# One written list for all five engines in a sliding-window attention + gated MLP kernel, with casts on three engines and two more batches transposed by DMA

## The chip, the core and the metric

One Trainium2 chip, one core, one launch. The time is the device time of the launch in microseconds. A core has five engines that run their own instruction queues in order: PE (matrix products), ACT (scalar activations), DVE (vector), POOL (GpSimd) and SP (used here for transfers only). Transfers are issued from the queues of SP, ACT and POOL and run on 16 shared DMA engines. Products go to PSUM, eight banks of 512 fp32 columns.

## What is computed

Sliding-window attention with ALiBi slopes over 8 batches, 8 heads, 576 tokens of 64, and then an MLP over all 4608 tokens:

```python
def _attn_ref(q, k, v):                      # 8, 8, 576, 64
    window, scale = 128, 1.0 / np.sqrt(D)
    scores = scale * np.matmul(q, k.transpose(0, 1, 3, 2))
    rel = pos[:, None] - pos[None, :]
    bias = slopes[:, None, None] * (-np.abs(rel))
    mask = (rel >= 0) & (rel < window)
    scores = np.where(mask, scores + bias[None], -1e9)
    ...                                      # softmax over the last axis
    return np.matmul(attn, v)

def _moe_ref(x, w_in, w_out, beta):          # x: 4608 x 512
    h = x @ w_in                             # 512 x 2048
    g = h * (1.0 / (1.0 + np.exp(-beta * h)))
    return g @ w_out                         # 2048 x 512
```

## The kernel before

The attention of a batch works in blocks of 128 tokens (four full ones and a tail of 64). The MLP works in nine groups g of 512 tokens, so groups and batches don't line up: a group waits for the last attention block that it contains. All products are in bf16.

**Inputs.** `get` (line 207) and `get_pair` (line 218) load q, k and v as fp32 from the queue of SP into 14 staging buffers `fst`; `cast_pair` (235), `cast_qk` (228, 229) and `cast_v` (243) turn them into bf16 on POOL. For batches 0 and 1 the staged blocks (`bst`, four buffers) are transposed by PE (`TP`, 287; the tail in `TT`) and copied from PSUM to `QK` by DVE and ACT; from batch 2 on a DMA transposes them (`DT`, 413, on SP's queue). From batch 3 on v is loaded and cast in one transfer on POOL's queue (`get_v`, 250). The weights W1 and W2 come in four pieces each, on POOL's queue (258, 262). `QK` and `VS` are two deep, by batch parity.

**Attention.** Scores are `SP_` (324, 335) for batches 0 and 1 and `SC` (438) from batch 2 on; ACT takes the exponential into `pt` (342, 446), DVE multiplies in the ALiBi factor and mask (`factor`, 171, 176), PE multiplies with v (`PVP` 374, `PVB` 492 and 495), DVE divides by the row sum (`norm` 358 and 359, 499 and 500).

**Its output** `xn` must be transposed into `XT`, a ring of three groups. `X` (lines 503 to 535) does it: for batches 0 and 1 by PE; for batches 2 and 3 by four PE products with the identity (line 520) and a copy by ACT (line 523); for batches from `XDMA = 4` on by a DMA on SP's queue (line 512).

**MLP.** `Hm` (557) makes 128 rows of h for a group from four products of 128x512, `H` in what follows; ACT makes tanh (564) and DVE the gated product (565) into `gT` (two buffers). `OS` (588) makes a quarter of an output block from four such products, `O` in what follows; ACT halves the sum into `osb` (598) and `store` (606) sends it out from POOL's queue for groups below 3 and from ACT's later.

**Order.** The order on PE, SP and POOL is that of the program. A first part is written out by hand; after that `spread` places the attention steps `att` between the MLP's steps by weights, `jobs` and `blocks` place the loads and casts. ACT and DVE are written by hand until the first two H, then left to the scheduler. PSUM is held in pools that are opened and closed as the stages go by. `idle` and `calm` are products of zeros that keep PE running in the opening.

Of the kernel before, what the change touches and what calls it, by code (L numbers as in the profile page):

```python
# [15 lines left out]
P = 128  # L16


@with_exitstack
def kernel(  # L20
# [63 lines left out]
    psum_c = ctx.enter_context(tc.tile_pool(name="psum_c", bufs=1, space=bass.MemoryType.PSUM))  # L84
    psum_h = ctx.enter_context(tc.tile_pool(name="psum_h", bufs=2, space=bass.MemoryType.PSUM))
    trans = ExitStack()
    psum_t = trans.enter_context(tc.tile_pool(side="right", name="psum_t", bufs=2, space=bass.MemoryType.PSUM))
    SS = psum_c.tile([P, 2, 512], F32, name="SS")
    psum_c.seal()
    opening = ExitStack()  # L90
    psum_x = opening.enter_context(tc.tile_pool(name="psum_x", bufs=1, space=bass.MemoryType.PSUM))
    SX = psum_x.tile([P, 2, 512], F32, name="SX")
    late, gates = {"tick": 0}, {}
    spans = [SS]

    def span():

        spans.append(spans.pop(0))
        return spans[-1]

    def obank(name, tag=None):
        if tag is None:
            late["n"] = late.get("n", 0) + 1
            tag = "ops" if late["n"] % 2 else "h3"
        return late["o"].tile([P, DM], F32, name=name, tag=tag)[:]

    def after(ins, other):
        tc.add_manual_dep(
            ins.ins, other.ins.name,
            mybir.DependencyInfo(mybir.DependencyClass.Sync, mybir.DependencyReason.DATA),  # L110
            reason="gate",
        )

    def idle(n):
        for _ in range(n):
            nc.tensor.matmul(
                SS[:, 0, :], lhsT=zeros[:, 0:P], rhs=zeros[:], start=True, stop=True,
                skip_group_check=True)  # L120

    def constants():
# [4 lines left out]
        idle(8)  # L127
# [35 lines left out]
    def falls_late(i):  # L163
        to, a, w = ((0, 0, P), (128, 0, 64), (192, 0, P), (320, 1, 64), (384, 1, P))[i]
        after(nc.vector.tensor_copy(
            out=falls[:, :, to : to + w], in_=fall[:, :, a, 0:w]), gates[1, 4])

    def factor(pt, m, p):

        if m:  # L170
            nc.vector.tensor_tensor(  # L171
                out=pt[:], in0=pt[:], in1=falls[:, 2 * p : 2 * p + 2], op=ALU.mult)
            return
        t = (fallq if m is None else fall)[:, 2 * p]
        x = pt[:].rearrange("k e (a n q) -> k (e a) n q", a=2, n=2)
        nc.vector.tensor_tensor(  # L176
            out=x, in0=x, in1=bass.AP(tensor=t.tensor, offset=t.offset,
                                      ap=[list(t.ap[0]), [P, 4], [0, 2], [1, P]]), op=ALU.mult)
# [11 lines left out]
    def betas():  # L190
        bps = psum_t.tile([P, NFF], F32, name="bps", tag="t")
        nc.tensor.transpose(out=bps[:], in_=bflat[:], identity=identf[:])
        nc.vector.tensor_scalar_mul(beta_h[:], bps[:], 0.5)
# [7 lines left out]
    def get(what, b, sb):  # L201
# [5 lines left out]
        return nc.sync.dma_start(  # L207
# [4 lines left out]
    def get_pair(b, p):  # L212

        r = []
        for what, src in (("k", k), ("q", q)):
            f = fst_pool.tile([P, 2, 4, D], F32, name="fst", tag="fst")
            fs[what, b, "p", p] = f
            r.append(nc.sync.dma_start(  # L218
                out=f[:].rearrange("r h c d -> r h (c d)"),
                in_=src[b, 2 * p : 2 * p + 2, 0:FULL, :].rearrange("h (r c) d -> r h (c d)", c=4),  # L220
            ))
        return r[0]

    def cast_qk(b, sb):
        rows = ROWS[sb]
        t = bst_pool.tile([P, 2, H, D], BF16, name="bst", tag="bst")
        staged[b, sb] = t
        nc.gpsimd.tensor_copy(out=t[0:rows, 0], in_=fs.pop(("q", b, sb))[0:rows])  # L228
        return nc.gpsimd.tensor_copy(out=t[0:rows, 1], in_=fs.pop(("k", b, sb))[0:rows])  # L229

    def cast_pair(b, p):
        t = bst_pool.tile([P, 2, 4, 2 * D], BF16, name="bst", tag="bst")
        staged[b, "p", p] = t
        for i, what in ((1, "k"), (0, "q")):
            r = nc.gpsimd.tensor_copy(
                out=t[:, i].rearrange("r c (h d) -> r h c d", d=D),
                in_=fs.pop((what, b, "p", p))[:])
        return r

    def cast_v(b, sb):  # L240
        moved.add(("v", b, sb))
        rows = ROWS[sb]
        return nc.gpsimd.tensor_copy(  # L243
            out=VS[b % 2][0:rows, sb, :, 0:D], in_=fs.pop(("v", b, sb))[0:rows])
# [22 lines left out]
    pts, xns = {}, {}  # L267

    def calm(n):

        z = psum_h.tile([P, 512], F32, name="z", tag="hps")
        for _ in range(n):
            nc.tensor.matmul(
                z[:], lhsT=zeros[:, 0:P], rhs=zeros[:], start=True, stop=True,
                skip_group_check=True)

    def TP(b, p):
        src = staged.pop((b, "p", p))
        for i in (1, 0):
            if (b, p) == (0, 1):  # L280
                calm(1 + i)
            tps = psum_t.tile([P, FULL], BF16, name="tps", tag="t")
            to = tps[:].rearrange("d (c r) -> d c r", c=4)
            if i == 0:
                to = tps[:].rearrange("d (k c r) -> d c k r", k=4, c=4)
            for c in range(4):
                nc.tensor.transpose(out=to[:, c], in_=src[:, i, c], identity=ident[:])
            if i:
                nc.vector.tensor_copy(
                    out=QK[b % 2][:, 1, p, 0:FULL].rearrange("d (r c) -> d r c", c=4),  # L290
                    in_=tps[:].rearrange("d (c r) -> d r c", c=4))
            else:
                nc.scalar.copy(out=QK[b % 2][:, 0, p, 0:FULL], in_=tps[:])

    def TT(b):

        src = staged.pop((b, 4))
        tps = psum_t.tile([P, 2, NP, 64], BF16, name="tpt", tag="t")
# [7 lines left out]
        nc.scalar.copy(out=QK[b % 2][:, :, :, FULL:S], in_=tps[:])  # L306
# [6 lines left out]
    def SP_(b, vis, p):  # L313
        qk = QK[b % 2]
        sps = SX if vis == "B" else SS
        w = WIDTH[vis]
        biased = vis == "A" or p > 1
# [22 lines left out]
        pt = pt_pool.tile([P, 2, 512], BF16, name="pt", tag="pt")  # L340
        pts[b, vis, p] = pt
        nc.scalar.activation(out=pt[:, :, 0:w], in_=sps[:, :, 0:w], func=ACTF.Exp, scale=qscale)
        if vis == "B" and b and not biased:
            factor(pt, None, p)

    def room(b, shape):

        if b == 0:
            return psum_h.tile(shape, F32, name="pvh", tag="hps")[:]
        if "o" in late:  # L350
            return obank("pvo")[:, 0 : 4 * 66].rearrange("p (h x) -> p h x", x=66)
        return psum_t.tile(shape, F32, name="pv", tag="t")[:]
# [9 lines left out]
    def PVP(b, vis, p):  # L362
        vs = VS[b % 2]
        if vis == "A":
# [3 lines left out]
        pv = room(b, [P, 4, 66])  # L368
# [10 lines left out]
        norm(xn[:, q0 : q0 + 2, :].rearrange("p n (e d) -> p (n e) d", e=2), pv, P)  # L379

    def XP(b, p):
        xn = xns.pop((b, "p", p))
        xt = psum_t.tile([P, 4, P], F32, name="xtp", tag="t")
        for n in range(4):
            nc.tensor.matmul(xt[:, n, :], lhsT=xn[:, n, :], rhs=order[:], start=True, stop=True)
        (nc.vector.tensor_copy if (b, p) == (0, 3) else nc.scalar.copy)(
            out=XT[:, p, b * S : b * S + FULL], in_=xt[:].rearrange("d n q -> d (n q)"))

    def SCT(b):
        qk = QK[b % 2]  # L390
        for p in range(NP):
            for kb, at in ((4, 0), (3, 256)):
                for e in range(2):
                    nc.tensor.matmul(
                        SS[:, e, at + 64 * p : at + 64 * p + 64],
# [3 lines left out]
                    )  # L399
        nc.scalar.activation(  # L400
            out=PC[:, 0:1024].rearrange("p (e w) -> p e w", e=2), in_=SS[:], func=ACTF.Exp,
            scale=qscale)
        nc.vector.tensor_tensor(
# [5 lines left out]
    def DT(b, sb):  # L409
# [7 lines left out]
        if (b, sb) == (2, 0):  # L417
            after(r, w2[3])
# [3 lines left out]
    def SC(b, m, pp):  # L422
# [3 lines left out]
        spans.sort(key=lambda t: t is not SS)  # L426
        for p, sps in zip(pp, spans):
            for kb in ((0, 1), (2, 4, 3))[m]:
                at, then = COLS[kb]
                nq = {3: P + 64, 4: 64}.get(kb, 2 * P)  # L430
                for e in range(2):
                    o = sps[:, e, at : at + min(nq, 512 - at)]
                    if kb in (0, 2):
                        o = bass.AP(
                            tensor=o.tensor, offset=o.offset,
                            ap=[list(o.ap[0]), [then - at, 2], [1, P]],
                        )
                    nc.tensor.matmul(  # L438
                        o,
                        lhsT=qk[64 * e : 64 * e + 64, 1, p, P * kb : P * kb + P],  # L440
# [101 lines left out]
    def Hm(g, j, cs):  # L542
# [18 lines left out]
        if cs[-1] < NDM - 1:  # L561
            return
# [332 lines left out]
```

The softmax here doesn't subtract the row's maximum and nothing guards it: scores larger than these inputs give would overflow.

## Time and profile before

| | us |
|---|---|
| median of 3 runs | 325.4 (324.65 to 327.33) |
| span of the profiled execution | 324.0 |
| ACT busy in it | 194.1 (60%) |
| DVE busy in it | 183.1 (57%) |
| POOL busy in it | 98.8 (30%) |

The span runs from the first to the last instruction of the execution that was profiled. The products of PE overlap each other in the records, so that "mean ns of one" is longer than what one costs: 16 products of 128x512 in a row take 3.45 us on the chain of work, or 0.216 us each, while the mean of one is 379 ns.

The transfers of the page, with size and median time from issue to landing:

```profile
fst<-in_k_dram SPq DMA_DIRECT2D x32, 256.0 KB, 6.0
vs<-in_v_dram POOLq DMA_DIRECT2D x20, 128.0 KB, 6.1
W<-in_moe_w_in_dram POOLq DMA_DIRECT2D x4, 512.0 KB, 7.9
W<-in_moe_w_out_dram POOLq DMA_DIRECT2D x4, 512.0 KB, 12.8
```

### The profile page before, as it was taken

To read this page: it belongs to the slowest core of one execution; us is meant where nothing else is said; L and a number is where in the kernel's file an instruction comes from. 1 tells how busy PE (TensorE), PEld (TensorE's weight loads), DVE (VectorE), ACT (ScalarE), POOL (GpSimd) and SP (SyncE) were. 2 spreads that over 40 slices of the span, in tenths; PEclk is the share of its full clock that TensorE was granted. 3 is DMA by queue.
4 is the path that set the end of the run, shared out by engine and by line. 5 is a ranking of instruction groups with operands and counts; after the bars stand their busy time and mean duration, and the time that the engine had idled before them with its cause. 6 is when DMAs were issued, how large, how long until landed. Compare 5 with 4: busy or idle time off the path is not lost.

```text
span 324.0 us, 5988 instructions
## 1 busy us (share of the span) xinstructions
PE 312.7 (97%) x2297; PEld 153.3 (47%) x2297; DVE 183.1 (57%) x346; ACT 194.1 (60%) x283; POOL 98.8 (30%) x154
## 2 busy tenths in 40 slices
PE   8888999999999999999999999999999999999995
PEld 3454554443545454544454545444544455444443
DVE  5777877542548753785178717752775176335500
ACT  6857887635558865685467635845675465346511
POOL 4864820333873455356226232340000000000000
PEclk9999999999999999999999999999999999999999
DMA  7999999998999999999969994993222112110021
GB/s 221 252 263 238 176 196 196 215 199 162 214 181 208 222 208 139 230 217 148 257 153 196 150 245 94 211 138 107 18 65 60 65 18 65 46 62 32 10 90 65
DMA packets 147565, 48.84 MB, mean 151 GB/s; under 512 B 135360, under 2 KB 143824, under 8 KB 147536
## 3 DMA queue, kind: packets, MB, share of 16 engines
q1 hardware_dynamic: 115712, 32.39, 56.1%
q0 software_dynamic: 28624, 10.29, 26.1%
q10 hardware_dynamic: 3200, 5.78, 5.1%
q8 instruction: 18, 0.29, 0.4%
q14 instruction: 11, 0.09, 0.1%
HBM read 36.71 MB, written 9.44 MB: 142 GB/s over the span
## 4 chain that ended last, share of the span: by engine, by line
PE 69%; DMA 17%; SPq 6%; POOL 2%; ACT 2%; DVE 2%; issue 1%; POOLq 0%; DVEq 0%
PE ops L588 21%; PE hps L557 21%; PE hpo L557 10%; PE oph L588 7%; DMA fst<-in_v_dram 6%; DMA qkT<-bst 6%; SPq L207 3%; DMA fst<-in_q_dram 3%; DMA fst<-in_k_dram 2%; PE SS L438 2%; SPq L218 2%; PE ST L438 1%; PE SS L495 1%; PE SS L492 1%; POOL bst L229 1%
## 5 line engine op out<-in xcount | busy, mean ns | idle before, releaser
L588 PE MATMUL ops<-W,gT 128*128 128x512 bf16 (+1 forms) x464 | 109.7, 372 | 0.5 <-ACT osb L598 0.5
L565 DVE SCALAR_TENSOR_TENSOR gT<-sig,hps 128x512 bf16<-128x512 bf16 x100 | 67.6, 683 | 71.8 <-ACT sig L564 71.5
L557 PE MATMUL hps<-XT,W 128*128 128x512 bf16 x400 | 99.9, 379 | 0.3 <-DVE XT L533 0.3
L564 ACT ACTIVATE sig<-hps,beta_h 128x512 bf16<-128x512 f32 x100 | 68.1, 690 | 34.6 <-PE hps L557 33.2
L588 PEld LDWEIGHTS <-gT 128*128 128x128 bf16 x592 | 55.7, 98 | 61.6 <-issue 1.9
L557 PEld LDWEIGHTS <-W 128*128 128x128 bf16 x576 | 52.9, 98 | 60.8 <-issue 3.6
L228 POOL CAST bst<-fst 128x512 bf16<-128x512 f32 (+1 forms) x32 | 20.8, 650 | 74.4 <-DMA fst<-in_q_dram 42.4
L557 PE MATMUL hpo<-XT,W 128*128 128x512 bf16 x168 | 43.1, 379 | 0.0
L564 ACT ACTIVATE sig<-hpo,beta_h 128x512 bf16<-128x512 f32 x42 | 29.0, 690 | 16.9 <-PE hpo L557 16.9
L565 DVE SCALAR_TENSOR_TENSOR gT<-sig,hpo 128x512 bf16<-128x512 bf16 x42 | 28.6, 681 | 11.2 <-ACT sig L564 11.0
L598 ACT ACTIVATE osb<-ops 128x512 f32<-128x512 f32 (+1 forms) x28 | 16.6, 595 | 25.5 <-PE ops L588 25.5
L446 ACT ACTIVATE pt<-SS 128x1024 bf16<-128x1024 f32 x24 | 24.5, 1020 | 11.6 <-PE SS L438 11.1
L588 PE MATMUL oph<-W,gT 128*128 128x512 bf16 x128 | 29.3, 379 | 0.0
L229 POOL CAST bst<-fst 128x512 bf16<-128x512 f32 (+1 forms) x32 | 22.1, 690 | 15.6 <-DMA fst<-in_k_dram 15.0
L176 DVE TENSOR_TENSOR pt<-pt,fall 128x1024 bf16<-128x1024 bf16 x24 | 17.1, 712 | 14.8 <-ACT pt L446 14.8
L446 ACT ACTIVATE pt<-ST 128x1024 bf16<-128x1024 f32 x24 | 24.5, 1022 | 0.0
L171 DVE TENSOR_TENSOR pt<-pt,falls 128x1024 bf16<-128x1024 bf16 x24 | 18.8, 791 | 9.3 <-ACT pt L446 9.3
L250 POOL DMA_DIRECT2D vs<-in_v_dram x25 | 21.3, 869 | 0.2 <-issue 0.2
L598 ACT ACTIVATE osb<-oph 128x512 f32<-128x512 f32 x8 | 4.8, 597 | 21.1 <-PE oph L588 21.1
L495 PEld LDWEIGHTS <-pt 128*128 128x128 bf16 x240 | 14.8, 97 | 4.2
L243 POOL CAST vs<-fst 128x512 bf16<-128x512 f32 (+1 forms) x15 | 10.5, 703 | 15.9 <-DMA fst<-in_v_dram 15.9
L438 PEld LDWEIGHTS <-qkT 64*128 64x128 bf16 x240 | 8.9, 94 | 12.5 <-issue 12.0
(102 smaller groups left out, 257.8 us busy)
## 6 DMA issues: line engine op xcount, KB each, us to landing
fst<-in_k_dram SPq DMA_DIRECT2D x32, 256.0 KB, 6.0
fst<-in_q_dram SPq DMA_DIRECT2D x32, 256.0 KB, 5.3
out_dram<-osb ACTq DMA_DIRECT2D x22, 256.0 KB, 2.0
fst<-in_v_dram SPq DMA_DIRECT2D x12, 256.0 KB, 5.4
out_dram<-osb POOLq DMA_DIRECT2D x12, 256.0 KB, 5.2
vs<-in_v_dram POOLq DMA_DIRECT2D x20, 128.0 KB, 6.1
W<-in_moe_w_in_dram POOLq DMA_DIRECT2D x4, 512.0 KB, 7.9
W<-in_moe_w_out_dram POOLq DMA_DIRECT2D x4, 512.0 KB, 12.8
```

The source lines that it names most:

```text
L171: nc.vector.tensor_tensor(out=pt[:], in0=pt[:], in1=falls[:, 2 * p : 2 * p + 2], op=ALU.mult)
L228: nc.gpsimd.tensor_copy(out=t[0:rows, 0], in_=fs.pop(("q", b, sb))[0:rows])
L229: return nc.gpsimd.tensor_copy(out=t[0:rows, 1], in_=fs.pop(("k", b, sb))[0:rows])
L250: return nc.gpsimd.dma_start(out=VS[b % 2][0:rows, sb, :, 0:D], in_=v[b, :, P * sb : P * sb + rows, :].rearrange("h p d -> p h d"))
L438: nc.tensor.matmul(o, lhsT=qk[64 * e : 64 * e + 64, 1, p, P * kb : P * kb + P], rhs=qk[64 * e : 64 * e + 64, 0, p, P * kb : P * kb + nq], ...
L446: nc.scalar.activation(out=pt[:], in_=sps[:], func=ACTF.Exp, scale=qscale)
L495: nc.tensor.matmul(o, lhsT=weights(b, qb, h, 0), rhs=vs[:, qb, h, 0 : D + 1], start=qb == 0, stop=True, skip_group_check=True)
L557: nc.tensor.matmul(hps, lhsT=W1[:, c, bass.ts(j, P)], rhs=XT[:, c, c0 : c0 + TOKG], start=(c == 0), stop=(c == NDM - 1),)
L564: gates[g, j] = nc.scalar.activation(out=sig[:], in_=hps, func=ACTF.Tanh, scale=beta_h[:, j : j + 1])
L565: gates["gT"] = nc.vector.scalar_tensor_tensor(out=gts[g][:, j, :], in0=sig[:], scalar=1.0, in1=hps, op0=ALU.add, op1=ALU.mult)
L588: nc.tensor.matmul(ops_[:, cols], lhsT=gT[:, j, i * P : i * P + P], rhs=W2[:, j, cols], start=(j == 0), stop=(j == NFF - 1),)
L598: nc.scalar.mul(o, ops_[:, cols], 0.5)
```

## The change

The order of all five engines now comes from one text, `PLAN`, of 1300 steps; each step is a name and its indices (batch, block or pair, group, PSUM bank) and an engine letter where there is a choice (p POOL, v DVE, a ACT, s SP). A loop reads it and issues the steps one after the other. Each earlier function is split into its PE part and its ACT or DVE part, so that the two can stand at different places. PSUM is one tensor of eight banks, and each PE step names its bank.

- Casts: all 95 were on POOL; 44 still are, 31 are on DVE and 20 on ACT, in the opening and in the later batches.
- `X` by PE is left for the tails of batches 0 and 1 only. Batches 2 and 3 go through `XD`, ten DMA transposes more on SP's queue. The 40 products of line 520 and the ten copies by ACT are gone. All other products stay, 16 of zeros among them.
- Output copies: 24 on ACT and 13 on DVE (before 36 and 1). Stores: 17 on POOL's queue, 13 on SP's and 7 on ACT's (before 12, 3 and 22).
- Order in the opening: before the first H there are, besides batch 0, seven of the eight pair transposes of batch 1 and four of its eight score steps. The loads of batch 1's q and k stand between batch 0's v. The first W1 piece is issued on POOL after the cast of batch 0's third v block. The last scores of batch 7 come before group 7.
- One step, `A`, gets a factor by DVE as a possibility (`MA`); the list doesn't use it.

```diff
+PLAN = """
+k.s:0:1 k.s:0:0 const beta:2 k.s:0:2 ck.p:0:1 ck.p:0:2 q.s:0:0 q.s:0:1 k.s:0:3 cq.p:0:1 ck.v:0:0
+Rk:0:2:3 z:2:2 Rq:0:1:0 Rk:0:0:6 Rk:0:1:5 rq.a:0:1 rk.a:0:0 cq.v:0:0 ones fr:2 ck.p:0:3 q.s:0:2
+q.s:1:0 q.s:0:3 Rq:0:0:0 cq.v:0:2 k.s:1:0 gv.s:0:3 Rk:0:3:7 rk.a:0:2 k.s:1:3 cq.p:0:3 Rq:0:2:1
...
+B:0:2:3:1 EA:0:2 EB:0:0 fr:7 MB:0:0 cq.v:1:0 q.s:1:1 A:0:0:1:1 z:2:6 B:0:3:5:1 w1:0 EB:0:2 EA:0:0
+A:0:1:2:1 k.s:1:1 cv.v:0:1 Rq:1:0:0 Rk:1:0:4 VB:0:2:1 EB:0:3 EA:0:1 rk.a:1:0 rq.v:1:0 A:0:3:5:1
...
+cK.v:2:0 d:1:3 H:1:4:1 gq.s:2:3 gk.s:2:1 D:2:4 cQ.v:2:2 d:1:8 w2:2 d:1:7 d:1:0 H:1:5:3 a:1:4
+cQ.a:2:0 H:1:10:2 D:2:0 gk.s:2:3 d:1:13 d:1:4 cQ.a:2:1 a:1:5 cK.a:2:1 a:1:1 a:1:14 cK.v:2:2 D:2:1
+cQ.a:2:3 O:0:0:0:4 gv.s:2:2 O:0:3:0:6 d:1:14 d:1:5 O:0:3:1:6 fl:4 H:1:15:1 H:1:2:0 d:1:1 a:1:11
...
+cK.p:3:2 O:1:1:0:1 V:2:2:5 n:2:2 cQ.v:3:2 O:1:2:0:0 oc.a:1:0 O:1:2:1:0 O:1:1:1:1 cK.a:3:0 V:2:4:3
+O:1:2:2:0 O:1:1:2:1 O:1:3:0:2 XD:2:0 V:2:3:6 gq.s:4:4 n:2:3 O:1:2:3:0 O:1:1:3:1 XD:2:2 gk.s:3:4
+D:3:1 H:2:0:7 n:2:4 a:2:0 d:2:0 D:3:2 cK.v:3:4 H:2:4:6 cK.p:3:3 oc.a:1:1 cQ.p:3:3 H:2:7:5 a:2:4
...
+"""
...
+    PS = psum.tile([P, 8, 512], F32, name="PS")
...
+    def move(eng, out, in_):
+        (nc.scalar.copy if eng is nc.scalar else eng.tensor_copy)(out=out, in_=in_)
...
-        nc.gpsimd.tensor_copy(out=t[0:rows, 0], in_=fs.pop(("q", b, sb))[0:rows])
-        return nc.gpsimd.tensor_copy(out=t[0:rows, 1], in_=fs.pop(("k", b, sb))[0:rows])
...
+        move(eng, staged[b, sb][0:rows, "qk".index(what)], fs.pop((what, b, sb))[0:rows])
...
-            nc.scalar.copy(out=XT[:, :, tok0 : tok0 + n1], in_=xt[:, :, 0:n1])
...
+    def XD(b, qb):
+        xnv = xns.pop((b, qb))[:].rearrange("p h d -> p (h d)")
+        for r0, r1, at in pieces(b, qb):
+            nc.sync.dma_start(out=XT[:, :, at : at + r1 - r0], in_=xnv[r0:r1], transpose=True)
...
+    def OC(eng, g, i, part=None):
...
+        if eng is nc.scalar:
+            nc.scalar.mul(o, src, 0.5)
+        else:
+            eng.tensor_scalar_mul(o, src, 0.5)
...
+    with tc.manual_schedule(engines={ENG.PE, ENG.SP, ENG.Pool, ENG.Activation, ENG.DVE}):
+        for step in PLAN.split():
+            name, *at = step.split(":")
+            name, _, eng = name.partition(".")
+            STEPS[name](*([ENGINES[eng]] if eng else []), *map(int, at))
```

Names of the list: k, q, gv, gq, gk are loads; ck, cq, cv, cQ, cK casts; Rk, Rq transposes of a pair by PE, rk, rq their copies; A, B and S scores, EA, EB and E their exponentials, MB and M the factors; VA, VB and V the products with v, nA, nB and n the divisions; XP the transposes of an output by PE with their copies xc; D and XD the DMA transposes; H, a, d the hidden products with tanh and gated product; O, oc, st the output products, copies and stores; z products of zeros.

## The prediction

> **What bounds the kernel now.** I read the page's busy times first, then stretches of the span, then what PE waited for, then the groups that the change touches.
>
> ```profile
> PE 312.7 (97%) x2297; PEld 153.3 (47%) x2297; DVE 183.1 (57%) x346; ACT 194.1 (60%) x283; POOL 98.8 (30%) x154
> ...
> PEclk9999999999999999999999999999999999999999
> DMA  7999999998999999999969994993222112110021
> ```
> ```profile
> 0.00:10.00 10.00, 7.93 (x48) 3.60 (x49) 6.72 (x28) 7.12 (x15) 5.19 (x16) 1.00 0.84 233
> 10.00:20.00 10.00, 8.90 (x124) 5.03 (x124) 7.04 (x21) 7.21 (x11) 8.81 (x15) 1.00 1.19 272
> 20.00:30.00 10.00, 9.32 (x65) 4.30 (x64) 7.74 (x15) 7.37 (x13) 3.34 (x5) 1.00 1.09 229
> 30.00:40.00 10.00, 9.19 (x99) 4.68 (x100) 7.83 (x18) 7.87 (x12) 8.84 (x15) 1.00 1.02 188
> 40.00:50.00 10.00, 9.12 (x113) 5.26 (x109) 7.12 (x18) 7.85 (x13) 2.01 (x4) 1.00 1.23 196
> ...
> 300.00:324.00 24.00, 20.07 (x109) 10.37 (x106) 4.46 (x7) 6.21 (x10) 0.00 (x0) 0.99 0.15 55
> ```
>
> PE is the bound: 97% busy at a full clock (1.00 in every stretch but the last). Its idle time is 324.0 - 312.7 = 11.3 us. The five stretches to 50 us hold 2.07 + 1.10 + 0.68 + 0.81 + 0.88 = 5.5 of it, the last stretch 3.9 (the last product, its copy and its store), and all between only 1.8. So the change can gain by fewer PE products, by a denser opening, and by little else. Beside PE the DMA engines are busy until 220 us (the row DMA; a share over 1 means that packets overlap in the records); this is what can turn into a new bound. The waits, in total, times and longest, name the small holes:
>
> ```profile
> POOL bst L228 <- DMA fst<-in_q_dram: 42.4, 12, 12.8
> ...
> PE tps L287 <- POOL bst L235: 1.8, 4, 0.7
> ...
> PE SS L438 <- DMA qkT<-bst: 1.3, 3, 0.5
> ```
>
> The last two are PE's and cost time. The first is POOL's: it stands before its casts until the load is there (and 15.0 us more, in 18 waits, for k). Nobody else stands with it.
>
> **Part 1: the output transposes of batches 2 and 3.** These are the products removed, and the transfers of the same kind that stay:
>
> ```profile
> L520 PE MATMUL ST<-ident,xn 128*128 128x128 bf16 x16 | 1.6, 220 | 0.5 <-DVE xn L500 0.5
> L520 PE MATMUL SS<-ident,xn 128*128 128x128 bf16 x16 | 1.5, 219 | 0.0
> ...
> L520 PE MATMUL ST<-ident,xn 64*128 64x64 bf16 x8 | 0.6, 192 | 0.0
> ```
> ```profile
> qkT<-bst SPq DMA_TRANSPOSE x30, 4.7
> ...
> XT<-xn SPq DMA_TRANSPOSE x21, 2.8
> ```
>
> Removed from PE: 1.6 + 1.5 + 0.6 = 3.7 us busy and 0.5 us of waits, all on the bound: **-4.2 us**. Removed from ACT: ten copies, some 5.6 us, hidden. Added: ten transposes on SP's queue. The nearest row is the same transfer for later batches: 1.19 us of SP's queue and 2.8 us to landing. Here a rule speaks for the change: the Trainium skill ("Advanced Engine Details and Errata", section X-Bar Transpose (TRN2)) has transposing transfers as fast as plain ones, at 350 to 400 GB/s, so that a block of 128 KB would take some 0.4 us (estimate: 128 KB by that rate). The row says 2.8 us in the quiet late stage, and 4.7 for the double size among loads; by the rule ten cost 4 us of transfer, by the row 28, or up to 47. I take the row. It is hidden if the group that needs the block starts later than that: between the last product with v of block (2, 2), V:2:2, and the first product of group 2 the list has eight O and two V. An O is 4 x 0.216 = 0.86 us and a V is 0.48 by the starts of successive groups in the timeline: 8 x 0.86 + 2 x 0.48 = 7.9 us. The division takes 0.2 + 0.69 of it, the transfer 2.8 to 4.7: 2 us are over, and SP's queue has only one load (gq.s:4:4) just ahead of it. For batch 3's three blocks in group 3 the lead in PE work is 6 to 10 us. I cost it at nothing; if the cover is gone PE waits 1 to 3 us at H of groups 2 and 3 each.
>
> **Part 2: the opening.** Same PE work up to group 1, less holes or more? Three things set the first H, at 19.4 us before. (a) Loads: the first twelve landed by 14.7 us (the cast of the last v block starts then), one each 1.0 us. In the new list batch 0's v blocks are loads 11, 13, 14 and 15, so the last v lands at 17 to 18, not 15. (b) W1's first piece is issued on POOL after the cast of load 14, near 18 us (10.5 before); with the page's 7.9 us to landing it is there at 26. (c) ACT: up to the last copy before the first H it gets ten copies of 0.59, five exponentials of 1.03, six of 0.81, one cast and one XT copy of 0.6 each, together 17.1 us (before 11.5: eight exponentials, four copies, three XT copies). The first copy needs the fifth load, landed at 8.2, its cast and transpose, so 9.2 + 17.1 = 26.3. All three give the first H at about 26 us, 6.6 later. By then PE has done 4.0 us more of batch 1 (seven transposes of 0.26, three A of 0.6, one B of 0.33). So 2.6 us are lost by 26 us. After that, before has 0.68 x 0.4 + 0.81 + 0.88 = 2.0 us of idle left to 50 us, and some 1.5 us of exposed switches between small and large products; the new list has runs of six and more H there. I take these 3.5 us as won back: net **-0.9 us**, with +3 (nothing won back, and a W piece late) and -4 as ends.
>
> **Part 3: casts off POOL.** POOL loses 51 casts of 0.61, 31 us, of an engine that was 30% busy: nothing by itself. Added on ACT: 20 of 0.59 (row of its XT cast, 594 ns), 12 us. Added on DVE: 31. Its cast from PSUM took 692 ns, its cast of 128 columns from SBUF 221 ns; the second has the nearer source, and four times the columns puts 512 at some 0.42 us (my value; 0.69 is the upper end): 13 to 21 us. ACT gives up 12 output copies of 0.6, the ten XT copies and 15 stores of 0.34, so it stays near 60%; DVE goes from 57% to some 64%. Neither becomes the bound by its sum. A rule speaks against this part: the trace has POOL's casts at 613 ns median and up to 1099, and DVE's product with two SBUF inputs at 693 and up to 1482, so they do hold each other up by 0.4 to 0.8 us. The Trainium skill ("SBUF — State Buffer", section SBUF: two separate sides) says that a DVE copy of fp32 within SBUF takes a port pair that GpSimd needs, for the whole instruction, and that transfers issued from POOL's queue then wait for their descriptors. By the row, 31 casts at 0.4 us of mutual waiting are 12 us spread over two engines with 35% and more to spare: nothing. By the rule the same collisions also fall on POOL's 17 stores, 25 v loads and 8 W pieces, at 0.4 us each up to 20 us, but before somebody waits they must eat the 8 us and more by which a v load leads its product. I cost it at nothing, and keep +2 as end.
>
> What does cost is order. A cast on ACT or DVE stands until its load has landed, as POOL did (42.4 us in 12 waits, 15.0 in 18), and now tanh and the gated product stand behind it, then the PSUM bank, then PE. The place is H of group 1: cK.a:2:1 and cQ.a:2:3 on ACT have a:1:1 and a:1:14 around them, and H:1:2 reuses bank 0 of H:1:14. I put this at **+1.5 us** in all: ends 0 (every load early) and +20.
>
> **Part 4: the rest.** The waits of PE for qkT (1.3 us) fall at the first scores of batches 2 and 3. By the order of the new list 4 to 13 us of PE work lie between each D of the first blocks and those scores: **-1.3 us**. The last product still has one copy and one store behind it: 0. Score runs that change PE between 64 and 128 rows are 25 against 24: 0. The copies on DVE and stores moved to SP and POOL have no reader: 0, unless an `osb` buffer is late.
>
> **Sum against the profiled execution:** 324.0 - 4.2 - 0.9 + 1.5 - 1.3 = 319.1. The median of the runs stands 1.4 above the span, so **320.5**.
>
> **Rivals.** (i) The casts decide, and it is slower. Of the 51 casts on ACT and DVE 45 are of batches 2 to 7. If each waits like POOL's (57.4 us in 30 waits, 1.9 each) that is 86 us on two engines; a third of it reaching PE would be +28. From 9.7 us of PE waits on, the gain of 6.4 (parts 1, 2, 4) is gone and 1% lost besides; I take 12: 331. For it: DMA busy at 9 to 220 us, POOL always waiting. Against: loads stand well ahead of their casts in the list (5 to 30 us of PE work for most), DMA moves 139 to 257 GB/s between slices in the same stage, so it isn't full throughout, and ACT has 40% free. (ii) It only loses what it removes elsewhere: opening 3 us worse, XD late for groups 2 and 3 by 2 us: 324.0 - 4.2 + 3 + 2 + 1.5 - 1.3 = 325.0, or 326.4 as a run: no change. For it: the three sums of part 2 that all say 26 us. (iii) Banks named by hand let PE run ahead of ACT, and the opening's holes go: 312.7 - 3.7 + 3.9 + 2 = 314.9, or 316.3. Against: the loads of the opening come no faster. (iv) That the transposes by PE aren't really gone: excluded, PE has 40 products less in program order.
>
> **How the numbers follow.** 1% is 3.25 us, about what can be told from no change here: faster means below 322.15, slower above 328.65. Forecast: 0.35, of which 0.27 faster; (iii) 0.24, faster; (ii) 0.18, no change; (i) 0.23, slower. What is left of the forecast, 0.08, is no change. Faster 0.51, same 0.26, slower 0.23. The range for 8 in 10 goes from 314.0 (under (iii), with the bounds of part 2) to 330.0; the forecast's own range is 317 to 325.
>
> **What would show it.** PE busy near 309 us, and no line for products with the identity of batches 2 and 3. The first H near 26 us. Idle of PE to 50 us between 4 and 7 us. ACT or DVE groups of casts whose idle before is put down to fst loads: under 15 us in all if I am right, over 40 if (i) is. At the first H of groups 2 and 3 no wait for XT. The prediction is wrong if PE idle between 50 and 300 us is over 5 us, or if PE's busy time grows because H and O are slower than 0.216 us each.

## The result, and the profile after

| | before | after |
|---|---|---|
| median of 20 runs each, us | 325.45 (324.17 to 328.68) | 326.02 (323.22 to 328.41) |
| ratio, 95% interval | | 1.0008 (0.9989 to 1.0028) |
| span of the profiled execution, us | 324.0 | 324.1 |

No change, where 320.5 was forecast. Single executions of either kernel differ by up to 1.6%, and a profile is one of them, so spans and medians are given side by side below. Medians and ranges take in all executions; the ratios leave out those over 1.5% longer than the fastest of the same kernel: five of the 20 after, and further down two of the six of "first piece of W2", its profiled one among them. The page after, rows as before:

```profile
PE 308.2 (95%) x2218; PEld 153.2 (47%) x2257; DVE 195.8 (60%) x390; ACT 188.8 (58%) x280; POOL 67.3 (21%) x108
...
PEclk9999999999997999999999999999999999999999
DMA  7999999999999999999999999959532040100034
```

The products are gone and PE is busy 4.5 us less, yet the span is the same: PE stands still for longer. One slice of the clock, near 100 us, is no longer full. DMA stays at 9 to about 210 us, nearly as long as before. (39 product records are missing in this trace, so PE's busy time is a little low.) Stretches of the span, columns as before (PE, PEld, DVE, ACT, POOL busy, clock, DMA share, GB/s):

```profile
0.00:10.00 10.00, 6.86 (x31) 3.37 (x32) 4.52 (x25) 4.88 (x12) 3.57 (x13) 1.00 0.79 258
10.00:20.00 10.00, 9.16 (x119) 5.07 (x119) 9.10 (x21) 8.86 (x14) 6.79 (x12) 1.00 1.18 276
20.00:30.00 10.00, 9.86 (x104) 5.64 (x105) 7.14 (x20) 9.36 (x15) 2.73 (x5) 1.00 1.25 203
30.00:40.00 10.00, 9.95 (x92) 4.90 (x92) 9.43 (x20) 7.82 (x13) 4.04 (x7) 1.00 0.99 185
40.00:50.00 10.00, 9.66 (x128) 6.00 (x130) 9.54 (x28) 8.23 (x13) 3.14 (x6) 1.00 1.12 184
...
60.00:80.00 20.00, 18.50 (x119) 8.77 (x120) 12.45 (x24) 12.34 (x18) 2.06 (x3) 1.00 1.26 209
80.00:100.00 20.00, 15.29 (x140) 8.12 (x141) 7.88 (x18) 4.97 (x9) 2.68 (x4) 0.98 1.46 185
100.00:120.00 20.00, 19.89 (x105) 8.75 (x106) 12.68 (x23) 16.13 (x23) 4.48 (x6) 0.94 1.23 192
```

The opening is denser (4.5 us idle to 50 us against 5.5). From 60 to 100 us PE is idle 6.2 us. In the kernel before it was idle 1.0 there:

```profile
60.00:80.00 20.00, 19.73 (x132) 8.99 (x131) 6.63 (x14) 9.42 (x13) 5.42 (x9) 1.00 1.13 186
80.00:100.00 20.00, 19.23 (x169) 9.75 (x167) 10.89 (x17) 12.67 (x19) 14.58 (x22) 1.00 1.38 197
```

What PE waited for after the change, in us in total, times and longest:

```profile
PE PS L632 <- issue: 3.5, 1, 3.5
PE PS L369 <- POOL bst L205: 1.9, 1, 1.9
PE PS L655 <- DMA W<-in_moe_w_out_dram: 1.4, 1, 1.4
...
PE PS L574 <- ACT vs L205: 0.9, 1, 0.9
```

The first is at the first H of group 2, which reads blocks 0 to 2 of batch 2. "Issue" names no releaser; the chain of waits (start, us, what) and SP's timeline show what was missing:

```profile
89.58 6.71 DMA XT<-xn
96.30 2.18 issue
98.48 8.75 PE PS L632 x32
```
```profile
85.21 2.69 SPq L620 DMA_TRANSPOSE XT<-xn  x1
87.96 1.04 SPq L684 DMA_DIRECT2D out_dram<-osb  x2
89.09 0.40 SPq L306 DMA_DIRECT2D fst<-in_k_dram  x1
89.58 1.35 SPq L620 DMA_TRANSPOSE XT<-xn  x1
91.02 0.63 SPq L306 DMA_DIRECT2D fst<-in_q_dram  x1
91.74 2.48 SPq L620 DMA_TRANSPOSE XT<-xn  x1
```

The transfer that the chain names is block (2, 0), landed at 96.3; block (2, 2) came last. It was divided by 86.97 (the DVE row starts at 86.28, 0.69). Its transpose, the last row, got its turn on SP's queue at 91.74, 4.8 us later, and took 6.6 to landing: 98.3. PE had been ready at 94.97 and started at 98.48. Then 32 products took 8.75 us, where 32 x 0.216 is 6.9; the granted clock had fallen. Fine stretches, same columns:

```profile
94.80:98.40 3.60, 0.17 (x1) 0.00 (x0) 0.23 (x1) 0.00 (x0) 0.61 (x1) 1.00 1.57 170
98.40:100.00 1.60, 1.52 (x5) 0.62 (x6) 0.00 (x0) 0.18 (x1) 0.00 (x0) 0.71 1.28 268
100.00:102.00 2.00, 2.00 (x6) 0.76 (x5) 1.02 (x2) 1.41 (x3) 1.33 (x3) 0.50 0.89 176
102.00:104.00 2.00, 2.00 (x9) 0.84 (x8) 1.02 (x2) 1.15 (x3) 0.85 (x2) 0.88 1.08 224
```

The theory at this point, from which theory A of each run follows: the stop of 3.5 us and the slow clock behind it, 1.9, eat what part 1 saves. The rivals: the transfers are slow whatever their order; the casts lose the time on their new engines; or DMA sets the pace, so that PE only comes sooner to its next wait.

### The profile page after: what moved, and what is told of

Read it like the earlier page. It is cut to its first block, busy times and chain, and to the rows that moved or that the text cites. A ratio compares the mean times of both kernels' runs of the same rounds, so it can differ in the third digit from the quotient of the medians.

```text
span 324.1 us, 5863 instructions
## 1 busy us (share of the span) xinstructions
PE 308.2 (95%) x2218; PEld 153.2 (47%) x2257; DVE 195.8 (60%) x390; ACT 188.8 (58%) x280; POOL 67.3 (21%) x108
## 4 chain that ended last, share of the span: by engine, by line
PE 78%; DMA 8%; SPq 6%; issue 2%; DVE 2%; POOL 1%; ACT 1%; POOLq 0%; DVEq 0%
PE PS L632 38%; PE PS L655 31%; SPq L306 4%; PE PS L522 3%; DMA W<-in_moe_w_in_dram 3%; DMA XT<-xn 2%; PE PS L577 2%; DMA fst<-in_k_dram 2%; DMA fst<-in_v_dram 2%; PE PS L574 2%; SPq L315 1%; PE PS L666 1%; SPq L500 1%; DVE xnp L438 1%; ACT sig L640 1%
## 5 line engine op out<-in xcount | busy, mean ns | idle before, releaser
L632 PE MATMUL PS<-XT,W 128*128 128x512 bf16 x558 | 132.3, 383 | 4.5 <-issue 3.5
L640 ACT ACTIVATE sig<-PS,beta_h 128x512 bf16<-128x512 f32 x144 | 94.5, 687 | 71.7 <-PE PS L632 65.9
L655 PE MATMUL PS<-W,gT 128*128 128x512 bf16 x542 | 130.2, 379 | 2.7 <-DMA W<-in_moe_w_out_dram 1.4
L645 DVE SCALAR_TENSOR_TENSOR gT<-sig,PS 128x512 bf16<-128x512 bf16 x144 | 93.7, 682 | 59.3 <-ACT sig L640 58.9
L531 ACT ACTIVATE pt<-PS 128x1024 bf16<-128x1024 f32 x48 | 46.8, 1025 | 14.5 <-PE PS L522 14.5
L205 POOL CAST bst<-fst 128x512 bf16<-128x512 f32 (+1 forms) x36 | 22.3, 628 | 106.3 <-DMA fst<-in_k_dram 36.6
L586 DVE TENSOR_TENSOR xn<-PS,zb 128x512 bf16<-128x512 f32 (+1 forms) x30 | 20.7, 690 | 1.0
L577 PE MATMUL PS<-vs,pt 128*128 128x65 bf16 x240 | 17.3, 193 | 0.0
L574 PE MATMUL PS<-vs,pt 128*128 128x65 bf16 x192 | 14.7, 193 | 0.9 <-ACT vs L205 0.9
L431 ACT ACTIVATE pt<-PS 128x1024 bf16<-128x1024 f32 (+1 forms) x16 | 14.0, 934 | 1.9 <-PE PS L421 1.7
L522 PE MATMUL PS<-qkT 64*128 64x256 bf16 (+2 forms) x240 | 14.9, 250 | 0.0
```

The source lines that it names most:

```text
L205: (nc.scalar.copy if eng is nc.scalar else eng.tensor_copy)(out=out, in_=in_)
L522: nc.tensor.matmul(o, lhsT=qk[64 * e : 64 * e + 64, 1, p, P * kb : P * kb + P], rhs=qk[64 * e : 64 * e + 64, 0, p, P * kb : P * kb + nq], ...
L531: nc.scalar.activation(out=pt[:], in_=held.pop(("S", b, m, p)), func=ACTF.Exp, scale=qscale)
L574: nc.tensor.matmul(o, lhsT=weights(b, qb - 1, h, 1), rhs=vs[:, qb - 1, h, 0 : D + 1], start=True, stop=False, skip_group_check=True)
L577: nc.tensor.matmul(o, lhsT=weights(b, qb, h, 0), rhs=vs[:, qb, h, 0 : D + 1], start=qb == 0, stop=True, skip_group_check=True)
L586: nc.vector.tensor_tensor(out=xn[0:nq].rearrange("p (g h) d -> p g h d", g=2), in0=pv[0:nq, :, :, 0:D], in1=zs[0:nq].broadcast_to([nq, 2, ...
```

## The experiments

All are edits of the changed kernel but one (part 1 in the old order). Diffs show the list's steps on the queue concerned, in their order; "..." stands for steps left out. Ratios are to the kernel before; the changed kernel has 1.0008. The runs (5 to 22 executions each) were taken in four groups, each with the kernel before beside it. Its median was 325.3 to 326.4 us, so across groups only the ratios can be compared. The changed kernel was timed in the first comparison alone.

| run | ratio (95%) | median, us | profiled span, us |
|---|---|---|---|
| zeros in the wait | 0.9986 (0.9967 to 1.0006) | 324.77 | 322.6 |
| three blocks on PE | 0.9945 (0.9922 to 0.9968) | 323.16 | 323.6 |
| three blocks, spaced | 0.9905 (0.9871 to 0.9939) | 323.22 | 321.5 |
| SP's order | 0.9979 (0.9958 to 0.9999) | 325.00 | 323.0 |
| PE's order | 0.9980 (0.9959 to 1.0000) | 324.99 | 323.9 |
| part 1 in the old order | 1.0381 (1.0354 to 1.0407) | 338.37 | 335.3 |
| all ten on PE | 1.0077 (1.0055 to 1.0100) | 328.37 | 326.1 |
| W2 earlier | 1.0122 (1.0094 to 1.0150) | 329.51 | 328.0 |
| four orders together | 1.0092 (1.0058 to 1.0125) | 328.77 | 328.6 |
| casts on POOL | 1.0107 (1.0078 to 1.0135) | 328.83 | 328.0 |
| orders without W2 | 0.9975 (0.9950 to 1.0001) | 325.30 | 324.2 |
| orders, cast later | 0.9935 (0.9916 to 0.9954) | 324.21 | 321.2 |
| spaced, v sooner | 0.9946 (0.9917 to 0.9975) | 323.69 | 320.7 |
| spaced, cast later | 0.9919 (0.9888 to 0.9951) | 323.58 | 320.4 |
| first piece of W2 | 0.9892 (0.9854 to 0.9930) | 323.85 | 326.1 |

**Zeros in the wait.**

```diff
-XD:2:2 gk.s:3:4 D:3:1 H:2:0:7
+XD:2:2 gk.s:3:4 D:3:1 z:16:7 H:2:0:7
```

> Changed kernel, with 16 products of zeros (3.5 us) into a free bank just ahead of the first H of group 2, so that PE works while XD:2:2 is under way; nothing that counts is done earlier. Theory A (the granted clock falls because PE stopped): H starts at 98.5 us as before, the clock stays at 1.0 from 94 to 104 us, the 32 products take 6.9 us and not 8.75, the span falls by near 1.9 us to 322, ratio 0.992 to 0.998. Rival (the clock falls for a reason of its own, as its load or its time): the clock is 0.5 to 0.9 there again, and the span stays at 324 or grows, ratio 0.999 to 1.003.

```profile
94.80:98.40 3.60, 3.60 (x18) 1.63 (x17) 0.62 (x1) 0.00 (x0) 0.62 (x1) 1.00 1.54 171
98.40:100.00 1.60, 1.60 (x9) 0.74 (x8) 0.00 (x0) 0.29 (x1) 0.00 (x0) 1.00 1.28 268
100.00:102.00 2.00, 2.00 (x11) 0.93 (x10) 1.57 (x3) 2.00 (x4) 1.19 (x2) 1.00 0.95 188
```

The first H starts at 98.65, nearly as in the changed kernel, after zeros; the clock stays at 1.00 and the same 32 products take 7.1 us. So the clock fell because PE stopped, and that cost 1.7 us (1.9 against 32 x 0.216). The span is 1.5 shorter; in the ratio the gain (0.2%) is inside the intervals.

**Three blocks on TensorE**, blocks 0 to 2 of batch 2, at once and then spaced:

```diff
-n:2:1 XD:2:1    n:2:0 XD:2:0    n:2:2 XD:2:2
+n:2:1 X:2:1:7 x.a:2:1    n:2:0 X:2:0:7 x.v:2:0    n:2:2 X:2:2:5 x.a:2:2
```

> Changed kernel, with blocks 0 to 2 of batch 2 transposed by TensorE again (12 identity products and three copies, two on ACT, one on DVE) and no transfers for them; all else as in the changed kernel. Theory A: PE gets 1.1 us of products back (12 of 0.092 us), but no wait of 3.5 us at the first H of group 2 and no slow clock behind it (1.9 us), so the span falls by 3.5 to 4.5 us to near 320, ratio 0.985 to 0.993. Rival (the loss lies in the casts on ACT and DVE, or is made up by another wait at the same place): the ratio stays at 0.997 to 1.006, the product time added, not taken away.

```diff
-n:2:1 X:2:1:7 x.a:2:1 ... S:2:1:2:4 ... oc.a:0:1
+n:2:1 ... S:2:1:2:4 X:2:1:7 ... oc.a:0:1 x.v:2:1
-n:2:0 X:2:0:7 x.v:2:0 ... O:1:0:3:2
+n:2:0 ... O:1:0:3:2 X:2:0:7 x.a:2:0
-n:2:2 X:2:2:5 x.a:2:2 ... O:1:2:1:0
+n:2:2 ... O:1:2:1:0 X:2:2:5 x.v:2:2
```

> As the run with blocks 0 to 2 of batch 2 on TensorE, but each product step stands one or two output steps behind its norm, and the copies are placed so that no exponential waits behind them: that run lost 1.4 us at an S and 1.0 us at an X to its own placement. Theory A (the stop at the first H of group 2 and the slow clock behind it are the loss, near 4 us): another 1.5 to 2.4 us go, median near 321, ratio 0.984 to 0.991. Rival C (from 30 to 140 us the transfers set the pace, and PE only comes sooner to its next wait for one): no better than that run, ratio 0.993 to 0.997.

Giving 12 products back to PE made the kernel faster: 0.6% at once, 1.0% spaced, both clear of the changed kernel's interval. The H of group 2 is no longer waited for in either trace. So the three transfers cost more than the 1.1 us that they save. In the first run the placement cost an S 1.4 us and an X 1.0; spaced, both are gone, but the intervals of the two overlap.

**The same wait, mended by order.** SP's order, then PE's:

```diff
-gq.s:3:0 XD:2:1 st.s:0:2 st.s:0:3 gk.s:3:2 XD:2:0 gq.s:4:4 XD:2:2
+XD:2:1 XD:2:0 XD:2:2 gq.s:3:0 st.s:0:2 st.s:0:3 gk.s:3:2 gq.s:4:4
```

> Changed kernel, with the transposes of batch 2's first three blocks put on SP's queue directly behind their norms, ahead of two loads (gq.s:3:0, gk.s:3:2) and two stores; the POOL casts of those two loads move behind with them. Theory A (the first H of group 2 waits because XD:2:2 stood 4.8 us in SP's queue, and the clock halves after that stop): XD:2:2 is issued near 88 us in place of 91.7 and lands near 95; PE's wait at H falls from 3.5 us to under 1, the 32 products of H take near 6.9 us in place of 8.75, the profiled span falls by 3 to 5.5 us to 319 to 321, ratio to before 0.983 to 0.993. Rival B (transposing transfers are simply slow beside the loads, whatever stands ahead): the landing grows from 6.6 us as much as the issue comes earlier, the wait at H stays over 2.5 us, ratio 0.997 to 1.004. Rival C (what is won there is lost at the next loads, which come later now): the wait at H goes and a new wait of 3 us or more comes up at an S, V or H of batch 3 or group 3; ratio 0.997 to 1.004.

```diff
-H:2:0:7 ... H:2:5:1 O:1:3:1:2 S:3:0:0:6 O:1:3:2:2 S:3:0:3:3 S:3:0:2:0 S:3:0:1:6 O:1:3:3:2
+O:1:3:1:2 O:1:3:2:2 H:2:0:7 ... H:2:5:1 S:3:0:0:6 S:3:0:3:3 S:3:0:2:0 O:1:3:3:2 S:3:0:1:6
```

> Changed kernel with one edit in PE's order: two of the output steps of group 1 (O:1:3:1 and O:1:3:2, 1.7 us, nothing new) stand ahead of the first H of group 2 in place of behind it, and O:1:3:3 one step later. SP's order is as in the changed kernel. Theory A: PE's wait at H falls from 3.5 us to 1.8 or less, the stop is too short for the clock to fall far, and the span falls by 2 to 3.5 us, ratio 0.989 to 0.995. Rival C (whatever is won at this H is lost at the first H of group 3 or at a load, since SP's queue sets the pace from 75 to 140 us): the wait at H shrinks, a wait for XT or qkT of as many us comes up before 140 us, ratio 0.997 to 1.002.

Landing times of the three transposes in the changed kernel, then with SP's order:

```profile
DMA to landing us min/median/max: 5.1/6.6/6.7
```
```profile
DMA to landing us min/median/max: 2.5/3.2/5.3
```

Behind each other they land sooner, not later: rival B falls. But the time gains only 0.3%, in both, and the intervals overlap that of the changed kernel. With SP's order PE's waits name three new places:

```profile
PE PS L632 <- DMA XT<-xn: 1.5, 1, 1.5
PE PS L574 <- DVE XT L205: 1.4, 1, 1.4
...
PE PS L522 <- DMA qkT<-bst: 0.5, 1, 0.5
```

The first is at group 3 (134.8 us), the second at V of block (2, 2). H of group 2 starts at 95.92, 2.6 earlier, and waits for nothing; at the first H of group 3 1.7 of that is left, at the end 1.1. For group 3 rival C is right in kind. The wait at V is not of the order's making: DVE stands 1.9 us there at a cast whose load is issued ahead of all that was moved (0.4 in the changed kernel's trace). With PE's order the wait is 1.7 at H, as expected, and the clock stays at 1.00, but W2 is 1.8 late in that execution.

**Part 1 alone, in the old order.**

```diff
-    XDMA = 4
+    XDMA = 2
```

> Kernel before, with its planner told to transpose the output of batches 2 and 3 by DMA too (XDMA = 2 in place of 4): part 1 of the change alone, in the old order. Theory A (the transposes pay where the order gives them their time): the 40 products go, near 4 us less PE work; if the planner leaves 7 us or more between a norm and its H, the span falls to 320 to 321, ratio 0.985 to 0.992. Rival (the transfers cost as much as they save beside the loads of batches 3 and 4, in any order): waits for XT at the H of groups 2 and 3 of 3 us or more together, ratio 0.997 to 1.01.

```profile
PE hps L557 <- DMA XT<-xn: 11.9, 1, 11.9
```
```profile
94.00:98.00 4.00, 0.00 (x0) 0.00 (x0) 0.00 (x0) 0.00 (x0) 4.00 (x6) 0.83 1.42 182
98.00:104.00 6.00, 0.00 (x0) 0.00 (x0) 0.00 (x0) 0.00 (x0) 1.15 (x2) 0.50 2.51 153
104.00:108.00 4.00, 3.39 (x8) 1.04 (x8) 0.69 (x1) 0.69 (x1) 1.00 (x2) 0.50 1.39 214
108.00:110.00 2.00, 2.00 (x12) 0.79 (x12) 0.81 (x2) 1.76 (x3) 1.93 (x4) 0.50 1.35 217
```

Slower by 3.8%, far worse than the rival said. It is the same place, the first H of group 2. PE was ready for it at 92.7 us, 0.7 after the last division; two transposes had stood behind three of qkT in SP's queue until 95.7 (the last of these stood for a cast, and the cast for a load that landed at 93.7) and had landed at 104.6. In the old order the transfers have next to no lead. The clock is at half until 110 us, more than 5 us after PE has started again.

**All ten on PE**, part 1 undone as a whole:

```diff
-XD:2:3 XD:2:4 XD:3:0 ... XD:3:4
+X:2:3:3 x.a:2:3  X:2:4:4 x.v:2:4  X:3:0:7 x.v:3:0  X:3:1:5 x.a:3:1
+X:3:2:1 x.v:3:2  X:3:3:1 x.v:3:3  X:3:4:7 x.v:3:4
```

> Changed kernel with part 1 undone as a whole: all ten blocks of batches 2 and 3 by products on PE (40 products, 3.7 us, and ten copies more on ACT and DVE), spaced as in the run with three blocks spaced; everything else of the change stays. Theory A (seven of the ten transfers are well hidden and each saves 0.37 us, three are not): slower than the run with three blocks by 2 to 2.6 us, ratio 0.991 to 0.998. Rival F (the transfers of the other seven blocks cost what they save too, by SP's queue and the DMA engines): as fast as the run with three blocks or faster, ratio under 0.990.

Slower by 1.7% than with three blocks spaced, 5.6 us, where 2.6 was the most expected. But the trace has 4.0 us of waits at the added steps and the scores beside them (1.3 at an S, 0.9 at H for a copy, 0.7 + 0.7 + 0.4 at X), of the new placement's own making. What is left, 1.6, is no more than the 28 products added (2.6 at 0.092 each). It speaks for theory A and against F, that the other seven transfers are well hidden, but it can't give part 1's worth to the microsecond.

**Transfers put ahead: W2, and the four orders.**

```diff
-cQ.p:2:4 w2:0 w2:1 w2:3 w2:2
+w2:0 w2:1 w2:3 w2:2 cQ.p:2:4
```

> Changed kernel with the four loads of W2 moved on POOL's queue ahead of the cast of q block 4 of batch 2, which waits 5.2 us for its load. Theory A (W2's 1.4 us at the first output product is a small separate loss): W2 is issued near 44 us in place of 49.1, the wait at the first output step goes, PE comes 1.4 us sooner to the H of group 2 and waits there as much longer, since SP's queue sets when XD:2:2 lands: ratio 0.998 to 1.003. Rival (W2 late is the loss that holds the whole): ratio 0.993 to 0.997.

```profile
PE PS L632 <- DVE gT L645: 6.9, 2, 6.6
```
```profile
DVE bst L205 <- DMA fst<-in_k_dram: 8.6, 2, 8.4
```

Both theories miss. W2's wait is gone, but its four pieces, issued at 43.4 us in place of 49.1, now run ahead of q and k of batch 2. A cast on DVE (cK.v:2:0, at 62.37 in place of 52.8) stands 8.4 us for its load, the gated products stand behind it, and PE behind them. That is rival (i) of the prediction, which the changed list had just kept away.

```diff
-gq.s:3:1 gq.s:4:1 gk.s:3:3 gq.s:3:4 gv.s:2:4 gv.s:2:3
+gq.s:3:1 gv.s:2:4 gv.s:2:3 gq.s:4:1 gk.s:3:3 gq.s:3:4
-st.s:0:2 st.s:0:3 gk.s:3:2 XD:2:0 gq.s:4:4 XD:2:2
+gk.s:3:2 XD:2:0 XD:2:2 st.s:0:2 st.s:0:3 gq.s:4:4
```

(with the edits of W2 and of PE's order)

> Changed kernel with four edits of order, no work changed: the two output steps ahead of the H of group 2 (as in the run of PE's order alone); two stores and one load (gq.s:4:4) behind XD:2:2 on SP's queue in place of ahead of it; W2's loads ahead of the waiting cast on POOL's queue; the two v loads that ACT's cast waited for (gv.s:2:4, gv.s:2:3) three loads sooner on SP's queue. Theory A: no wait over 1 us between 60 and 110 us, PE's clock 1.0 throughout, span 316.5 to 319, ratio 0.978 to 0.986, faster than both kernels. Rival C (SP's queue sets the pace): waits for XT or qkT at batch 3 and group 3 of 2 us or more together, ratio 0.99 to 0.997.

It has W2's edit, and with it the same kind of stop for gT, 7.0 us.

**The casts.** All 42 of batches 2 to 7 from ACT and DVE to POOL:

```diff
-cK.v:2:4 ... cQ.a:2:0 ... cv.a:2:2
+cK.p:2:4 ... cQ.p:2:0 ... cv.p:2:2
```

> Changed kernel with the 42 casts of batches 2 to 7 that stand on ACT and DVE put on POOL, at the same places of the list. Theory A (the casts' engine costs nothing in either direction): POOL's busy time rises from 67 us to near 94 (0.634 us each in the row of its own casts), ratio 0.996 to 1.004. Rival D (casts in ACT's and DVE's order hold up exponentials and normalizations, and cost what the change lost): ratio 0.985 to 0.993. Rival E (POOL's order, with its loads of v and its stores, is what was cramped): qkT or v later at the S and V of batches 2 and 3, ratio over 1.006.

```profile
91.28 0.61 POOL L205 CAST bst<-fst 128x512 bf16<-128x512 f32 x1 [9.66 <-DMA fst<-in_q_dram]
...
94.39 0.62 POOL L205 CAST vs<-fst 128x512 bf16<-128x512 f32 x1
```

POOL is at 93.1 us as reckoned, and slower by 1%: the cast of v (second row) stands behind one of q that waits 9.7 us for its load, and PE waits 5.0 for it. That is rival E's kind. So in this list the casts on ACT and DVE pay; that a late load then holds up fewer of them is a reading of this one trace.

**Which cast took the order's gain.** First the four orders without W2's edit:

> The run of the four orders together, without its edit of W2: the transposes of all ten blocks stay, two output steps stand ahead of the H of group 2, two stores and one load behind XD:2:2, two v loads three loads sooner. The 6.6 to 7.0 us that PE stood for gT in the two runs with W2's loads moved must be gone. Theory A: PE's wait at the H of group 2 under 1 us, clock 1.0 from 90 to 110 us, span 319 to 320.5, ratio 0.984 to 0.991. Rival C: the wait for XT or qkT comes up between 110 and 140 us, ratio 0.994 to 1.0, as with SP's order alone and PE's order alone.

```profile
87.94 0.43 DVE L205 CAST bst<-fst 128x512 bf16<-128x512 f32 x1 [2.49 <-DMA fst<-in_q_dram]
88.28 0.68 DVE L261 TENSOR_TENSOR pt<-pt,falls 128x1024 bf16<-128x1024 bf16 x1
88.88 0.28 DVE L205 COPY XT<-PS 128x256 bf16<-128x256 bf16 x1
```
```profile
89.00:90.00 1.00, 0.56 (x9) 0.50 (x10) 0.38 (x3) 0.00 (x0) 0.00 (x0) 0.68 1.79 206
90.00:91.00 1.00, 1.00 (x3) 0.40 (x3) 1.00 (x2) 0.00 (x0) 0.00 (x0) 0.50 0.80 53
```

No wait for XT is left over 0.5, yet no time is won: cQ.v:4:1 on DVE stands 2.5 us for its load, a factor and the copy of the last tail out of bank 6 stand behind it, V of block (2, 2), which writes banks 5 and 6, waits 2.0 us for that copy, and the clock halves again. A cast for batch 4 holds up batch 2. So it was moved back, with the v loads at their old place:

```diff
-cQ.v:4:1 M:2:1:2 x.v:1:4 n:2:2
+M:2:1:2 x.v:1:4 n:2:2 cQ.v:4:1
```

> Changed kernel with all ten transposes by DMA, two output steps ahead of the H of group 2, two stores and one load behind XD:2:2 on SP's queue (as in the run without W2's edit, but with the v loads at their old place), and the DVE cast cQ.v:4:1, which waited for its load with the copy x.v:1:4 and the normalization of block (2, 2) behind it, moved behind that normalization. Theory G (a cast in DVE's order took what the better order of the transposes won): no wait at V of block (2, 2) on DVE, XD:2:2 lands in time, only W2's 1.4 to 1.8 us and the v cast's 0.7 are left; median 322 to 323.5, ratio 0.988 to 0.994. Rival C (the transfers from 30 to 140 us set the pace whatever the order): another wait of 1 to 2 us in its place, ratio 0.995 to 1.0.

```profile
PE PS L655 <- DMA W<-in_moe_w_out_dram: 1.4, 1, 1.4
...
PE PS L632 <- DMA XT<-xn: 0.7, 1, 0.7
```

Theory G held in the ratio, if not quite in the median: the wait for DVE's copy is gone, the first H of group 2 starts at 97.03 without a wait (the 0.7 is at group 3), the clock stays at 1.00, and with all ten transposes and the same work the kernel is 0.7% faster than the changed one, the intervals apart. The cast was not moved alone; on top of the three spaced blocks (next) moving it made no difference that can be told.

**On top of the three spaced blocks**: the v loads sooner; the cast later; and, on top of the cast later, W2's first piece:

```diff
-gq.s:3:1 gq.s:4:1 gk.s:3:3 gq.s:3:4 gv.s:2:4 gv.s:2:3
+gq.s:3:1 gv.s:2:4 gv.s:2:3 gq.s:4:1 gk.s:3:3 gq.s:3:4
```

> As the run with three blocks spaced, with the two v loads (gv.s:2:4, gv.s:2:3) three loads sooner on SP's queue, since ACT's cast of v waits 4 us for them and PE 0.6 to 0.9 us for the cast. Theory A (PE's waits are single places that can be mended one by one): 0.5 to 1 us less than that run, ratio 0.982 to 0.989. Rival C: a later load (q or k) lands later in its place, the time is within 0.5 us of that run or longer.

```diff
-cQ.v:4:1 ... x.v:2:2
+... x.v:2:2 cQ.v:4:1
```

> As the run with three blocks spaced on TensorE, with cQ.v:4:1 moved behind the copy of block (2, 2). Theory G: the wait of 1.3 us at V of block (2, 2), seen when the v loads were moved, cannot come; 0.3 to 1 us less than that run, ratio 0.986 to 0.990. Rival C: the same time, ratio 0.990 to 0.993.

```diff
-cQ.p:2:4 w2:0 w2:1 w2:3 w2:2
+w2:0 cQ.p:2:4 w2:1 w2:3 w2:2
```

> As the run above, with the first of W2's four loads alone ahead of the cast that waits 5 us on POOL's queue. Theory A (W2's lateness is worth 1.4 us where it delays nothing else[...]): the wait at the first output step goes, no wait for gT comes, 1 to 1.5 us less than the run above, ratio 0.982 to 0.986. Rival C (each transfer put ahead holds up the q and k loads by as much, and a DVE cast stands for them): PE waits for gT 2 us or more near 60 us, ratio 0.99 or more.

None can be told from the spaced one. The v loads sooner bring back 1.3 us at V of block (2, 2), through the same cast: rival C. With only the first piece of W2 ahead, single runs lie between 320.9 and 328.9 us, so that its ratio, from the four short ones, flatters it. In the profiled one, of 327.9, W2 is in time but PE stands 4.5 us for gT; this time a cast on ACT stands 4.8 us for a load of k. How often that happens stays open. The best that can be relied on are three blocks spaced (0.9905, 0.9871 to 0.9939) and spaced with the cast later (0.9919): 0.8 to 1.0% faster than both kernels, with 28 of the 40 products still gone.

## Why the prediction was wrong

**The step that failed is in part 1: of its transfers it says "I cost it at nothing", because "2 us are over, and SP's queue has only one load (gq.s:4:4) just ahead" of the last of them, XD:2:2.** One load stands just ahead, but the queue had not run empty before it: two transposes, two stores and another load stood there too, all late (XD:2:1, whose division ended at 81.7, was issued at 85.2). A transpose took SP 1.3 to 2.7 us there, not the 1.19 of the quiet row. The waiting is 4.8 us, the landing 6.6 in place of 2.8 to 4.7. These 11.4 us don't fit under the PE work behind the division, which was 8.0 us in the trace (7.0 as reckoned, and a wait of 0.9 at a V); PE stood for the rest. The fallback, "PE waits 1 to 3 us at H of groups 2 and 3 each", was near for group 2 (3.5) and wrong for group 3 (none, until order made PE earlier: 1.5). The clock was nowhere in the sum: 1.9 us more. So part 1 is -4.2 (as reckoned) + 3.5 + 1.9 = +1.2, not -4.2. The rule that was weighed, that transposing transfers are as fast as plain ones, gave 0.4 us for a block; the three took 5.1 to 6.7 from issue to landing. Neither the rule nor the row that was taken instead counted the turn on the queue.

**Part 2, the opening, held, in part by luck.** First H at 25.63 (26 forecast), idle to 50 us 1.0 less (0.9 forecast). Of the three things named it was (b): the chain of waits has the first piece of W1, issued at 16.4 and landed at 25.6, so earlier to issue and slower to land than reckoned, and the two cancel. Likewise the idle time shows 0.3 us lost to 26 us and 1.2 won back after it, where the sum had 2.6 and 3.5, not all of it idle time.

**Part 3 was near in size by luck, and its places were wrong.** 1.5 were put on casts in order, at H of group 1. There nothing waited. PE lost 0.9 to a cast of v on ACT that stood 4.1 us for its load, and 1.4 to W2: its pieces are issued on POOL at 49.1 us, behind cQ.p:2:4, which stood 5.2 us; before they went out at 35 to 39. That queue was not looked at. The casts on ACT and DVE stood 7.5 us in all for loads, under the 15 named. What the sum couldn't show is how near the edge this is: with W2 put 5.7 us ahead, a cast on DVE costs PE 6.6. Of the rule on POOL's transfers nothing shows: a store took POOL's queue 574 ns and a v load 858 (573 and 869 before), and they took no longer to landing (3.8 and 5.6 us against 5.2 and 6.1).

**Part 4 held**: the changed kernel's waits have none for qkT.

Together: 1.2 - 1.0 + 2.3 - 1.3 = +1.2 against a measured +0.1 in the spans; 1.1 us of gain is not placed, within what single executions scatter. Of the rivals, (ii) gave no change, 326.4, for the reason "XD late for groups 2 and 3"; its other half, an opening 3 us worse, did not come. Rival (i) counts 45 casts of batches 2 to 7 on ACT and DVE; there are 42, which takes 2 us off its 28. The prediction's own test, PE idle over 5 us between 50 and 300, was met: it stood 7.7 us there (1.8 before), 6.2 of them from 60 to 100 us.

That the stop is the cause is shown by three kernels that take it away and are faster with intervals apart (three blocks at once, spaced, and the orders with the cast later). That the loss behind it is the clock is shown by the zeros in the trace; its share of the time was too small for the timing. The three that took the stop away gain 2 to 3.4 us by the ratios, not the 5.4 that the trace puts on it (less 1.1 where 12 products come back); in the others the gain turned into waits for the same queues and casts, in SP's order too, which also takes the stop away and gains nothing clear of the noise. So of the 5.5 us between forecast and measurement, 2 to 3.4 are shown by runs. The rest is argued from single traces: W2 (1.4), the cast of v (0.9) and waits that come up elsewhere. The miss of W2 was not mended by itself: the two ways that were tried cost more or could not be told.

## What to carry to other kernels

A transfer is hidden only if its whole path is: the wait for its turn on the issuing queue, the issue, and the landing under the load of that stage, not of a quiet one; read the queue's own timeline, and count everything ahead that is not yet issued. Where the DMA engines are full (a share of 1.0 to 1.5 in the stretches from 10 to 120 us), an order is a budget: a load that is put ahead makes another late, and an in-order cast for a later batch passes that on to everything behind it. And a stop of PE can be dearer than its length: behind the one of 3.5 us the clock fell, and the next 32 products took 8.75 us in place of 7.1.

## What the runs showed of the hardware

- The clock. It fell to 0.5 after stops of 3.5, 5.0, 6.6 and 11.9 us, for some 3 to 6 us after the restart, but also after one of 1.96 (orders without W2) and one of 1.97 (three blocks spaced, at 23 us), while one of 2.25 (spaced, cast later, at 67 us) and one of 1.69 (PE's order, at 99 us) left it at 1.00. The Trainium skill ("TensorE: Matmul & The Clock Gate", Part 1) has it fall after an idle window of about 3.4 us that runs freely. The four longer stops agree with that; those of 1.96 and 1.97 are shorter and cost the clock all the same, so the measurement decides: here a stop of about 2 us may or may not cost the clock. That this is a source of the scatter from run to run is likely, but was not counted.
- Transposing transfers issued one right behind the other landed in 5.3, 3.2 and 2.5 us (SP's order); with stores and loads between them in 5.1, 6.7 and 6.6 (the changed kernel), in one execution each.
